# A new order for a hand-scheduled kernel, with 43 DMA transposes instead of 35

## The chip, the core and the metric

The kernel runs on one core of a Trainium2 chip. The core's engines work side by side, each through its own queue in order: TensorE (PE) for matrix products and transposes, VectorE (DVE), ScalarE (ACT) and GpSimd (POOL) for work on elements, and SyncE (SP), which here only issues DMAs. ACT issues DMAs too. An engine that waits for a semaphore holds up all that stands behind it in its queue. The metric is the device time of one execution in microseconds (us). Runs of this kernel lie within about 0.5% of each other.

## What is computed

There are two phases. The first is a recurrent attention with decay; its output, with the heads laid side by side, is the x of the second, a mixing of tokens and channels. Batch 4, 8 heads, 768 positions, head width 64, so x is 4 x 768 x 512.

```python
for t in range(S):
    state = gamma * state + einsum('bhd,bhe->bhde', k[:, :, t], v[:, :, t])
    y[:, :, t] = scale * einsum('bhd,bhde->bhe', q[:, :, t], state)
x = y.transpose(0, 2, 1, 3).reshape(B, S, H * D)
theta = x @ w_theta
zr, zi = x * cos(theta), x * sin(theta)
u = x + einsum('ts,bsd->btd', w_tok_r, zr) + einsum('ts,bsd->btd', w_tok_i, zi)
out = u + maximum(u @ w_ch, 0)
```

The inputs and the output are float32 in HBM; the products are taken in bfloat16.

## The kernel before

The program is a list of short steps, each named by a token in a string, `ORDER` (L23 to L86). The last lines walk through the list and call one function for each token, so the order within each engine's queue is the order of that engine's tokens in the string. Between engines only data and buffers order the work: a token's place among tokens of other engines says nothing of its time. A letter at the end of a token chooses the engine: p for POOL, v for DVE, a for ACT, s for SP's queue.

```python
    for token in ORDER:
        name, *args = token.split(".")
        ops[name](*(int(x) if x.isdigit() else x for x in args))
```

**Attention, 24 units.** A unit n is a batch (n // 6), 256 positions and half of the heads; two units in a row are the two halves of the heads, and three such pairs make a batch. Lk, Lq and Lv (L157) load 256 KB each. ck casts k to bfloat16, cq and cv scale q and v by their decay (L279, L285). k and q must then be transposed, both into the tile kqT: either on PE (Tk and Tq, four transposes each, L293), with E copying the result out of PSUM, or by one DMA of SP, Dk (L309), which reads SBUF and writes SBUF. G.n is PE's main block: the scores of unit n (A, L323), the products of the unit before with its masked scores (Y, L393), and what the unit adds to the state (ST, L351). m.n masks the scores on DVE (L332). SU (L363 to L367) updates the state, SB copies it into bfloat16, and I.n multiplies q with it (L380). XA on ACT (L413) copies a finished part of x, transposed, to SBUF.

**Mixing, 24 tiles C or t of 128 positions** (six of them to a batch). Tx and Ex turn x back by PE and a copy (L427), or Dx does it by DMA (L434). Hh is theta = x @ w_theta (L441), CN its cosine and sine on ACT (L448), z their products with x (L455). Lth and cth bring in w_theta; Lw, cw, Tw and Ew load, cast and transpose the token weights. M.t.s is one part in six of the sum over positions of tile t (L488); it needs z of tile s of the batch. u adds x (L495). Then u is transposed: Tu and Eu by PE and a copy (L500), or Du by DMA (L510). O is u @ w_ch (L515), f adds the rectified product (L521), and SO stores 256 KB (L526). The last tile is cut into halves (Mh, uh, Tuh, Euh, Oh, fh, SOh). warm.n issues n products with zeros while PE has nothing to do.

**Buffers.** kqT has four buffers, uT three, raw loads nine of each kind, and the PSUM banks of most results are single. A transpose by DMA takes a buffer when it is issued, so Du.t waits until the product O that used that buffer is done. The bank of y (M) is single up to t = 17: M.(t+1).0 waits for u.t.

The DMA transposes of the three kinds, which the change touches:

```python
        nc.sync.dma_start_transpose(
            out=kqT.rearrange("p w a j t -> p (w a j) t"),
            in_=st["kqb", n].rearrange("p w d -> p (w d)"))
```

The string ORDER is all that the change edits. The functions that the tokens call are these:

## Time and profile before

| | us |
|---|---|
| median of three runs (169.21 to 170.32) | 170.04 |
| the profiled execution | 170.49 |
| its span, first to last instruction | 168.8 |

| engine | busy in the span, us | share |
|---|---|---|
| PE, matrix products | 156.0 | 92% |
| PE, weight loads | 89.0 | 53% |
| DVE | 123.8 | 73% |
| ACT | 79.2 | 47% |
| POOL | 78.5 | 47% |

The page of the profile has the busy time of each engine, also in 40 slices of the span (4.2 us each), the chain of work that ended last, and groups of like instructions with their mean duration. Queries to the trace give the same for a stretch of time, a line or a tile, a list in order of time, and for DMAs the time from issue to landing. "A <- B" behind an engine's wait names what it waited for. In a group, "128x512 bf16<-128x512 f32" is what is written and read, "x24" the number of instructions. SPq is SP's queue. Matrix products overlap, so a group's mean duration is longer than the distance from one to the next: a product of 128 x 512 has a mean of 379 ns and starts every 0.22 us.

Of the 35 DMA transposes 10 are Dk (units 12, 13, 14, 16, 17, 19 to 23), 11 Dx (tiles 6, 13 to 16, 18 to 23) and 14 Du (tiles 8 to 19, 21, 22). All stand on SP's queue, with the loads and 16 of the 23 whole-tile stores; seven stores are on ACT's.

### The profile page before, as it was taken

The page shows a single profiled execution, that of the slowest core. Times are in us where ns is not written, and L with a number is a line of the kernel's source. Part 1 is how long each engine was busy: PE and PEld are TensorE (multiplying, and loading weights), DVE is VectorE, ACT ScalarE, POOL GpSimd, SP SyncE. Part 2 cuts the span into 40 slices and gives each one's busy share as a digit, 9 for nine tenths or more (in the row PEclk, how much of TensorE's full clock was granted, in tenths as well). Part 3 has the DMA queues.
Part 4 walks back from the last instruction along what each step waited for, and adds up shares of the span by engine and source line. Part 5 has one row for each costly group of instructions (what it writes and reads, how often), then busy time and mean ns, then how long its engine had stood idle before and what let it go on. Part 6 is the DMA issues. An engine that isn't in the chain of part 4 may idle for free.

```text
span 168.8 us, 4924 instructions
## 1 busy us (share of the span) xinstructions
PE 156.0 (92%) x2017; PEld 89.0 (53%) x2044; DVE 123.8 (73%) x200; ACT 79.2 (47%) x159; POOL 78.5 (47%) x99
## 2 busy tenths in 40 slices
PE   7988794989899989999999999999999999999991
...
DMA  4999999999799999999999188899998736335555
GB/s 141 296 290 332 329 322 289 274 319 350 257 283 329 221 232 292 254 207 309 305 244 227 65 188 209 124 276 168 269 230 133 197 62 186 93 93 194 88 188 186
DMA packets 68582, 38.20 MB, mean 226 GB/s; under 512 B 25936, under 2 KB 63056, under 8 KB 68560
## 3 DMA queue, kind: packets, MB, share of 16 engines
...
## 4 chain that ended last, share of the span: by engine, by line
PE 65%; DVE 14%; SPq 11%; DMA 4%; issue 2%; ACT 1%; DVEq 0%; ACTq 0%
PE y_ps L488 31%; PE o_ps L515 11%; PE th_ps L441 9%; SPq L157 9%; DVE z L455 5%; DMA qf<-in_q_dram 4%; DVE at L332 3%; PE at_ps L323 3%; PE r_ps L393 2%; PE r_ps L380 2%; PE y_ps L538 2%; DVE kqb L279 1%; PE kq_ps L293 1%; PE w_ps L472 1%; SPq L185 1%
## 5 line engine op out<-in xcount | busy, mean ns | idle before, releaser
L488 PE MATMUL y_ps<-z,wtr 128*128 128x512 bf16 x135 | 51.2, 379 | 1.0 <-DVE z L455 0.5
L488 PE MATMUL y_ps<-z,wti 128*128 128x512 bf16 x129 | 48.9, 379 | 0.4 <-issue 0.3
L413 ACT CAST xT<-r_ps 128x256 bf16<-128x256 f32 x48 | 16.9, 372 | 30.7 <-PE r_ps L351 19.6
L279 POOL TENSOR_TENSOR kqb<-qf,qsc 128x512 bf16<-128x512 f32 x20 | 23.7, 1189 | 14.1 <-DMA qf<-in_q_dram 13.7
L332 DVE TENSOR_TENSOR at<-at_ps,mask 128x1024 bf16<-128x1024 f32 x24 | 29.1, 1213 | 1.1 <-PE at_ps L323 1.0
L521 DVE SCALAR_TENSOR_TENSOR ot<-o_ps,u 128x512 f32<-128x512 f32 x23 | 15.8, 689 | 14.9 <-PE o_ps L515 14.8
L441 PE MATMUL th_ps<-wth,xT 128*128 128x512 bf16 x89 | 25.0, 395 | 1.4 <-POOL wth L139 1.0
L285 POOL TENSOR_TENSOR vb<-vf,vsc 128x512 bf16<-128x512 f32 x17 | 18.9, 1114 | 10.0 <-DMA vf<-in_v_dram 9.9
L515 PE MATMUL o_ps<-wch,uT 128*128 128x512 bf16 x88 | 23.2, 379 | 0.4 <-DVE wch L139 0.2
L488 PEld LDWEIGHTS <-wti 128*128 128x128 bf16 x138 | 13.5, 98 | 13.4 <-issue 1.1
L448 ACT ACTIVATE cs<-th_ps,halfpi 128x512 bf16<-128x512 f32 x24 | 16.5, 688 | 8.2 <-PE th_ps L441 5.8
L488 PEld LDWEIGHTS <-wtr 128*128 128x128 bf16 x138 | 13.5, 98 | 13.0
L495 DVE TENSOR_TENSOR u<-y_ps,x_sb 128x512 bf16<-128x512 f32 x23 | 15.8, 686 | 5.8 <-PE y_ps L488 5.8
L448 ACT ACTIVATE cs<-th_ps,zerob 128x512 bf16<-128x512 f32 x24 | 16.2, 687 | 5.7 <-PE th_ps L441 5.3
L455 DVE TENSOR_TENSOR z<-cs,x_sb 128x1024 bf16<-128x1024 bf16 x18 | 16.6, 936 | 2.9 <-ACT cs L448 2.7
L455 POOL TENSOR_TENSOR z<-cs,x_sb 128x1024 bf16<-128x1024 bf16 x6 | 12.9, 2153 | 6.6 <-DMA x_sb<-xT 3.9
L139 POOL CAST kqb<-kf 128x512 bf16<-128x512 f32 x16 | 10.6, 666 | 8.3 <-DMA kf<-in_k_dram 6.1
L441 PEld LDWEIGHTS <-xT 128*128 128x128 bf16 x96 | 9.0, 100 | 10.3 <-issue 1.8
L515 PEld LDWEIGHTS <-uT 128*128 128x128 bf16 x92 | 8.7, 98 | 9.5 <-issue 0.3
L137 ACT COPY uT<-u_ps 128x512 bf16<-128x512 bf16 x6 | 3.5, 589 | 21.3 <-PE u_ps L500 21.3
L258 PE MATMUL y_ps<-zero 128*128 128x512 bf16 x36 | 12.0, 447 | 1.4 <-DVE zero L194 1.3
L293 PE MATMUL kq_ps<-ident,kqb 128*128 128x128 bf16 x112 | 9.8, 223 | 2.2 <-DVE kqb L279 2.2
...
## 6 DMA issues: line engine op xcount, KB each, us to landing
...
```

The source lines that it names most:

```text
L157: queues[e].dma_start(out=t.rearrange("p h a d -> p h (a d)"), in_=src[b, h * HU:(h + 1) * HU, i * 2 * P:(i + 1) * 2 * P, :].rearrange("h ...
L279: engines[e].tensor_mul(in_blocks(kqb_of(n)[:, 1]), by_token(raw["qf", n]), _bcast_last(K["qsc"][:, i, :, h * HU:(h + 1) * HU], D))
L285: engines[e].tensor_mul(in_blocks(vb), by_token(raw["vf", n]), _bcast_last(K["vsc"][:, i, :, h * HU:(h + 1) * HU], D))
L332: nc.vector.tensor_mul(at.rearrange("p g j a t -> p (g j) (a t)"), st["at_ps", n].rearrange("p g j a t -> p (g j) (a t)"), _bcast_mid(K["m ...
L413: nc.scalar.copy(st["xT", 2 * i + c][:, 2 * h:2 * h + 2].rearrange("p j (t a) -> p j t a", a=2), st["R", n + 1][:, c, :2 * P].rearrange("p ...
L441: nc.tensor.matmul(th_ps, st["xT", C][:, j, :], K["wth"][:, j, :], start=(j == 0), stop=(j == 3))
L448: nc.scalar.activation(st["cs", C][:, w, :], st["th_ps", C], AF.Sin, bias=K["zerob" if w else "halfpi"], scale=1.0)
L455: engines[e].tensor_mul(st["z", b][:, c], st["cs", C], _bcast_mid(x_of(C), 2))
L488: nc.tensor.matmul(st["y", t], K["wT"][r][:, s0, t0 * P:(t0 + 1) * P], st["z", b][:, s0, r, :], start=(s0 == 0 and r == 0), stop=(s0 == nT ...
L495: nc.vector.tensor_add(st["u", t], st["y", t], st["x", b][:, t0, :])
L515: nc.tensor.matmul(o_ps, st["uT", t][:, j, :], K["wch"][:, j, :], start=(j == 0), stop=(j == nD - 1))
L521: nc.vector.scalar_tensor_tensor(st["ot", t], st["o", t], 0.0, st["u", t], ALU.max, ALU.add)
```

## The change

The order is another one throughout; no function is changed, so the arithmetic is the same. What changes besides the places of the tokens:

| | before | after |
|---|---|---|
| k and q by DMA (Dk) | 12, 13, 14, 16, 17, 19 to 23 | 6, 11 to 15, 17 to 23 |
| x by DMA (Dx) | 6, 13 to 16, 18 to 23 | 11, 12, 14, 16 to 23 |
| u by DMA (Du) | 8 to 19, 21, 22 | 2, 3, 6 to 22 |
| stores SO on SP / ACT | 16 / 7 | 7 / 16 |
| SB on DVE / ACT / POOL | 18 / 23 / 7 | 7 / 25 / 16 |
| ck on DVE / ACT / POOL | 3 / 5 / 16 | 6 / 13 / 5 |
| cv on DVE / POOL | 7 / 17 | 4 / 20 |
| z on DVE / POOL | 18 / 6 | 16 / 8 |
| E on DVE / ACT | 8 / 6 | 6 / 5 |
| Ew on DVE / ACT | 8 / 4 | 6 / 6 |
| products with zeros | 40 | 48 |

The core of the diff, with the stretches that the prediction speaks of:

```diff
...
-const1 const2 const4 const3 const7 warm.8 Lk.0.s Lq.0.s ck.0.p Lv.0.s Lk.1.s const6 Lq.1.s Lv.1.s
-Lk.2.s cv.0.v Lq.2.s ck.1.a cq.0.p Tk.0 warm.4 Tq.0 E.0.v warm.4 G.0 const5 cq.1.v Lv.2.s SU.0
...
-cth.3.a SU.2 cq.4.p cth.2.p SB.2.0.v SB.2.1.v Lk.5.s warm.2 Tk.4 Tq.4 Ex.1.v Lq.5.s Lw.0.0.s
-cth.1.a warm.2 I.2 E.4.v G.3 SU.3 XA.2.1 cth.0.p SB.3.1.a Tx.0 warm.3 Hh.0 SB.3.0.v cv.4.p XA.2.0
-I.3 m.3 cq.5.v CN.0.1 ck.5.p Lv.5.s CN.0.0 cw.0.0.p Ex.0.v Lk.6.s G.4 Tk.5 SU.4 Tq.5 m.4 Lq.6.s
-Lw.1.0.s Hh.1 SB.4.0.a SB.4.1.p E.5.v XA.3.1 Tw.0.0 Lv.6.s cv.5.p Lk.7.s Lq.7.s Ew.0.0.v XA.3.0
-I.4 CN.1.0 Tx.3 ck.6.a G.5 cq.6.v Tq.6 Lv.7.s Lk.8.s CN.1.1 Lq.8.s z.0.p SU.5 SB.5.1.p Tk.6
-cw.1.0.p cv.6.p Lw.0.1.s m.5 Lv.8.s Ex.3.a XA.4.1 Hh.3 XA.4.0 ck.7.p Tx.2 cq.7.p Lk.9.s E.6.v
-Lq.9.s Hh.2 Ex.2.v CN.3.0 ck.8.p SB.5.0.a z.1.v Lw.1.1.s Tw.1.0 Lv.9.s Ew.1.0.v CN.3.1 cq.8.p I.5
-cv.7.p CN.2.0 z.3.v cv.8.p G.6 XA.5.1 Tk.7 XA.5.0 Hh.5 Lk.10.s Tq.7 Tk.8 CN.2.1 m.6 CN.5.1 Lq.10.s
-CN.5.0 SU.6 Hh.4 E.7.v SB.6.1.a Tq.8 SB.6.0.a Tx.4 M.0.0 I.6 cw.0.1.a G.7 z.2.v E.8.v Ex.4.v Tx.5
...
-M.2.1 cq.11.v cq.12.p cv.10.v SU.9 Lv.12.s Lk.13.s Tk.11 XA.8.1 SB.9.1.v M.2.2 Tq.11 cv.12.p M.2.3
-M.2.4 SB.9.0.v ck.13.p Tw.0.3 Dx.6 Lw.0.5.s Lw.1.5.s m.9 M.2.5 Dk.12 E.11.a Tw.1.3 I.9 Lq.13.s
-Lv.13.s cw.0.5.p Ew.0.3.v G.10 Lk.14.s Lq.14.s Ew.1.3.a Tu.0 u.2 SU.10 Eu.0.v M.3.0 M.3.1
-SB.10.0.a Tu.1 cw.0.4.a cw.1.4.v Lv.14.s Lk.15.s Eu.1.v SB.10.1.v M.3.2 XA.9.0 m.10 M.3.3 cch.3.v
-Tx.7 XA.9.1 cq.13.p M.3.4 Ex.7.a M.3.5 Tw.1.4 I.10 Tw.0.4 cch.1.a cch.0.a Dk.13 G.11 Ew.1.4.v
-cch.2.v u.3 Tu.2 O.0 SU.11 Ew.0.4.a ck.14.p Tu.3 cv.14.p XA.10.0 M.4.0 Eu.2.a m.11 M.4.1 f.0
-Eu.3.v z.6.v M.4.2 M.4.3 Lq.15.s SB.11.0.a O.1 M.4.4 cq.14.p XA.10.1 SB.11.1.a M.4.5 Tw.0.5 f.1
...
-Lv.18.s u.5 M.6.0 m.12 M.6.1 CN.10.1 M.6.2 cv.15.p CN.11.1 cq.16.p Ex.10.v I.12 G.13 CN.11.0 M.6.3
-z.10.v Tu.5 XA.12.1 z.11.v Eu.5.a M.6.4 SU.13 M.6.5 SB.13.0.v O.3 u.6 Tu.4 M.7.0 ck.17.p M.7.1
-M.7.2 Dk.16 M.7.3 M.7.4 SB.13.1.a f.3 M.7.5 m.13 Tk.15 Tq.15 XA.12.0 Eu.4.a Lk.19.s E.15.a I.13
-u.7 Lq.19.s G.14 XA.13.0 M.8.0 m.14 SU.14 Lv.19.s XA.13.1 M.8.1 SB.14.0.v M.8.2 SB.14.1.a M.8.3
...
-SO.4.s cv.17.v CN.13.0 z.13.p Eu.6.a I.16 cv.20.p G.17 Dk.19 O.7 SU.17 f.7 Tx.12 SB.17.0.a Tq.18
-Tk.18 Dx.15 M.10.4 XA.16.1 Ex.12.a Lk.21.s O.6 z.12.p XA.16.0 SB.17.1.v ck.20.a M.10.5 cv.19.v f.6
-m.17 SO.5.s u.10 I.17 Hh.15 E.18.a O.8 Du.9 G.18 XA.17.0 f.8 Dx.16 SU.18 ck.21.p Dk.20 Lq.21.s
-M.11.0 m.18 M.11.1 CN.15.1 CN.15.0 cq.21.p M.11.2 Hh.14 Lv.21.s M.11.3 SB.18.0.a XA.17.1 Du.10
-M.11.4 SB.18.1.a Lk.22.s Lq.22.s cq.22.p z.15.v ck.22.p I.18 M.11.5 SO.7.s CN.14.0 G.19 CN.14.1
-Hh.16 u.11 Tx.17 Dk.21 M.12.0 XA.18.0 SU.19 CN.16.0 z.14.v M.12.1 SB.19.0.a Du.11 Hh.17 M.12.2
-M.12.3 Lv.22.s Ex.17.v CN.16.1 XA.18.1 CN.17.0 m.19 SB.19.1.a z.16.v CN.17.1 O.9 I.19 SO.6.s G.20
...
-Du.13 M.20.4 u.22 u.18 M.19.0 O.15 M.17.0 M.19.1 SO.16.a M.17.1 f.15 SO.14.s M.19.2 Du.22 M.19.3
-M.17.2 M.17.3 O.13 f.13 M.17.4 M.17.5 u.17 M.19.4 SO.12.s Du.18 O.18 M.21.0 M.21.1 f.18 M.19.5
-O.22 u.19 Du.17 M.21.2 M.21.3 f.22 SO.15.s M.21.4 Du.19 SO.13.a M.21.5 u.21 Du.21 O.17 M.20.5 f.17
-Mh.0.0 u.20 Mh.0.1 Mh.1.0 Mh.0.2 Mh.0.3 SO.18.a Mh.0.4 Mh.0.5 uh.0 O.19 Tu.20 Mh.1.1 SO.22.s f.19
-Mh.1.2 Eu.20.a Mh.1.3 Mh.1.4 Mh.1.5 uh.1 SO.17.s Tuh.0 O.20 Euh.0 f.20 Tuh.1 O.21 SO.19.s Euh.1
-Oh.0 Oh.1 f.21 SO.20.a SO.21.a fh.0 SOh.0 fh.1 SOh.1
...
+const1 const2 const4 const3 const7 warm.8 const5 Lk.0.s Lq.0.s Lv.0.s Lk.1.s Lq.1.s Lv.1.s cq.1.p
+cq.0.v ck.0.a warm.3 Tq.0 cv.1.p ck.1.a Lk.2.s Lq.2.s Lv.2.s Tk.0 const6 warm.4 Tk.1 E.0.v cv.0.v
+warm.2 G.0 SU.0 SB.0.1.a ck.2.a SB.0.0.a Tq.1 warm.7 I.0 Tk.2 m.0 E.1.v cv.2.v warm.1 G.1 Lk.3.s
+ck.3.a Lq.3.s cq.2.v Lv.3.s SU.1 XA.0.0 SB.1.0.a cq.3.p warm.3 Tq.2 Lk.4.s m.1 Lq.4.s Lv.4.s
+SB.1.1.a Tk.3 cv.3.p E.2.v XA.0.1 warm.5 I.1 cq.4.p ck.4.v Tq.3 Lth.s warm.2 G.2 SU.2 Lk.5.s
+SB.2.1.p m.2 XA.1.0 E.3.a SB.2.0.p Lq.5.s cv.4.p warm.2 Tx.0 Ex.0.a Lv.5.s warm.2 Tk.4 Lk.6.s
...
+SU.3 E.4.v Lv.6.s Lk.7.s XA.2.1 cq.6.p XA.2.0 warm.5 Tq.5 Lq.7.s SB.3.0.a SB.3.1.v m.3 ck.6.v I.3
+ck.5.a G.4 m.4 Lw.0.0.s SU.4 Ex.1.a SB.4.0.v XA.3.0 Hh.1 CN.0.0 ck.7.p CN.0.1 Lw.1.0.s Tk.5 Lv.7.s
+Tx.2 XA.3.1 cq.7.p E.5.v cv.6.p SB.4.1.a I.4 CN.1.0 Dk.6 G.5 CN.1.1 Lk.8.s Lw.0.1.s XA.4.1 z.0.v
+SU.5 Lq.8.s XA.4.0 Ex.2.v SB.5.0.p Lw.1.1.s SB.5.1.a Tx.3 Hh.3 cw.0.0.p CN.3.1 Ex.3.v Tk.7 CN.3.0
+cw.1.0.p Hh.2 m.5 I.5 Tq.7 cv.7.p Lv.8.s Lk.9.s G.6 E.7.a ck.8.a z.1.v SU.6 Tw.0.0 m.6 Lw.0.2.s
+Ew.0.0.v SB.6.0.p Tw.1.0 XA.5.1 Ew.1.0.a Lq.9.s Hh.5 SB.6.1.p z.3.v XA.5.0 Tx.4 CN.2.1 I.6
+cw.0.1.p Ex.4.v CN.2.0 Tx.5 cq.8.p CN.5.0 G.7 CN.5.1 cw.1.1.p Ex.5.v Hh.4 Tk.8 Lv.9.s Tq.8 M.0.0
+Tw.1.1 z.2.v CN.4.1 SU.7 XA.6.1 SB.7.1.p SB.7.0.v cv.8.p CN.4.0 Lk.10.s M.0.1 cw.0.2.p E.8.v
+XA.6.0 m.7 z.4.v M.0.2 cq.9.p M.0.3 I.7 Tw.0.1 Ew.1.1.a G.8 ck.9.a cv.9.p Ew.0.1.v Tw.0.2 M.0.4
+Lq.10.s XA.7.1 Tk.9 Lw.1.2.s z.5.v Lv.10.s SU.8 SB.8.1.v ck.10.p Lw.0.3.s XA.7.0 Tq.9 Ew.0.2.a
+E.9.a Hh.6 Hh.7 M.0.5 m.8 SB.8.0.a CN.7.0 u.0 cw.1.2.v Lk.11.s Lw.1.3.s I.8 CN.7.1 cq.10.p Lch.s
+Lq.11.s Tx.7 G.9 M.1.0 cv.10.v Tx.6 M.1.1 cw.0.3.a Ex.7.v SU.9 M.1.2 SB.9.0.p XA.8.1 Lv.11.s M.1.3
...
+cw.0.4.p Eu.0.a cch.2.v CN.6.1 cch.1.a Tw.1.3 XA.9.0 M.2.0 M.2.1 M.2.2 M.2.3 Lk.13.s Ew.1.3.v
+Tw.0.3 cq.12.p ck.11.a SU.10 Ew.0.3.a SB.10.1.a m.10 M.2.4 M.2.5 Tu.1 Dk.11 u.2 XA.9.1 O.0 Tx.8
+Eu.1.a M.3.0 Lq.13.s M.3.1 z.6.v Ex.8.a M.3.2 Tx.9 Lv.13.s SB.10.0.a ck.12.v f.0 Tw.0.4 z.7.v
+cw.1.4.a Lw.0.5.s Lw.1.5.s Ex.9.v Ew.0.4.v cv.12.p Lk.14.s M.3.3 M.3.4 M.3.5 cq.13.p I.10 ck.13.a
+O.1 G.11 Dk.12 Tw.1.4 f.1 Hh.9 u.3 XA.10.0 SU.11 cv.13.p Ew.1.4.a cw.0.5.v cw.1.5.p SB.11.0.v
+XA.10.1 CN.9.0 CN.9.1 m.11 Hh.8 M.4.0 Tw.0.5 M.4.1 Lq.14.s ck.14.a M.4.2 Ew.0.5.v Du.2 SB.11.1.p
+Tw.1.5 I.11 CN.8.1 CN.8.0 M.4.3 Dk.13 Lv.14.s G.12 XA.11.1 M.4.4 Ew.1.5.a m.12 SU.12 M.4.5 cq.14.v
+u.4 z.9.p SB.12.1.p SB.12.0.a Lk.15.s Hh.11 cv.14.p XA.11.0 O.2 Tx.10 I.12 G.13 M.5.0 Lq.15.s
+Dk.14 M.5.1 M.5.2 Dx.11 XA.12.0 m.13 CN.11.1 SU.13 M.5.3 z.8.p CN.11.0 SB.13.1.a f.2 M.5.4 Du.3
+M.5.5 SB.13.0.a u.5 XA.12.1 Lv.15.s Hh.10 CN.10.1 I.13 G.14 Ex.10.v cq.15.p ck.15.v CN.10.0 M.6.0
...
+Dk.15 O.3 cq.16.p Tu.4 M.7.0 cv.15.p M.7.1 SB.14.0.a Lk.17.s M.7.2 SB.14.1.a Lq.17.s m.14 f.3
+M.7.3 Eu.5.a Lv.17.s Lk.18.s Lq.18.s SO.0.a Tk.16 Eu.4.v cv.16.p XA.13.0 I.14 Lv.18.s SO.1.s G.15
+M.7.4 M.7.5 Lk.19.s O.4 Tq.16 XA.14.1 SU.15 Tx.13 u.7 SB.15.1.a M.8.0 cv.17.p m.15 f.4 cq.17.v
+M.8.1 E.16.a XA.14.0 SB.15.0.a M.8.2 M.8.3 M.8.4 Lq.19.s ck.17.p I.15 G.16 SU.16 O.5 SO.2.s M.8.5
+f.5 Hh.13 u.8 Dk.17 XA.15.1 Hh.12 Ex.13.v m.16 SB.16.1.p M.9.0 cq.18.p Tx.15 SO.4.a SB.16.0.p
+M.9.1 XA.15.0 M.9.2 CN.13.0 Du.7 M.9.3 CN.12.0 Du.6 cq.19.p I.16 CN.12.1 ck.19.v G.17 M.9.4 SO.3.a
+Dx.12 M.9.5 CN.13.1 u.9 ck.18.p Hh.15 SU.17 O.7 cv.18.p Du.8 M.10.0 M.10.1 Dk.18 f.7 SB.17.1.a
+M.10.2 Ex.15.v z.12.p O.6 Lv.19.s SB.17.0.a XA.16.0 M.10.3 XA.16.1 Lk.20.s m.17 f.6 I.17 Lq.20.s
+G.18 z.13.p SU.18 Lv.20.s XA.17.1 O.8 M.10.4 f.8 Dk.19 Dx.14 CN.15.0 ck.20.a Dx.17 XA.17.0 m.18
+SB.18.0.a CN.15.1 cv.19.p M.10.5 Hh.17 SB.18.1.v Hh.14 cq.20.p I.18 u.10 G.19 z.15.p CN.14.0
+M.11.0 CN.14.1 SU.19 m.19 Lk.21.s Dk.20 SB.19.1.a M.11.1 M.11.2 Dx.16 M.11.3 XA.18.0 SB.19.0.a
+Lq.21.s Lv.21.s cv.20.p ck.21.p Du.9 z.14.v M.11.4 M.11.5 Du.10 XA.18.1 u.11 CN.17.1 Lk.22.s I.19
+Hh.16 cq.21.p SO.5.a G.20 M.12.0 CN.16.0 XA.19.1 CN.16.1 M.12.1 Hh.19 m.20 z.16.v M.12.2 Dk.21
...
+u.14 I.21 M.16.0 m.21 f.11 M.16.1 M.16.2 ck.23.a M.16.3 Lv.23.s cv.22.p cq.23.p Dx.18 M.16.4 Dx.19
+M.16.5 Dk.23 Hh.18 u.16 G.22 SU.22 cv.23.v CN.18.0 M.15.0 SB.22.1.p CN.18.1 Du.12 XA.21.1
+SB.22.0.v m.22 M.15.1 z.19.p M.15.2 Du.16 Hh.21 SO.9.a SO.8.s XA.21.0 I.22 Hh.20 G.23 CN.20.0 m.23
+CN.20.1 Dx.20 M.15.3 SU.23 z.18.p SO.11.s M.15.4 Dx.21 XA.22.0 M.15.5 SO.10.a O.16 XA.22.1 M.20.0
+u.15 f.16 SB.23.1.a Du.14 SB.23.0.p M.13.0 M.13.1 O.12 f.12 I.23 CN.21.0 M.13.2 CN.21.1 G.24
+z.20.v XA.23.0 M.13.3 XA.23.1 z.21.v M.13.4 M.20.1 Dx.23 M.20.2 M.22.0 Hh.22 M.22.1 M.13.5 Hh.23
...
+M.19.0 M.19.1 O.15 M.19.2 M.17.0 f.15 M.17.1 M.19.3 Du.18 M.17.2 M.17.3 O.13 f.13 M.19.4 SO.15.a
+Du.22 M.17.4 M.17.5 SO.14.a O.18 M.19.5 u.17 f.18 u.19 Du.17 M.20.5 M.21.0 SO.13.a O.22 M.21.1
+f.22 SO.18.a M.21.2 SO.22.a Du.19 M.21.3 O.17 M.21.4 u.20 M.21.5 f.17 Du.20 O.19 u.21 Mh.0.0 f.19
+Mh.1.0 Mh.1.1 Mh.0.1 Du.21 Mh.1.2 Mh.1.3 Mh.1.4 Mh.1.5 uh.1 Mh.0.2 Mh.0.3 Mh.0.4 Mh.0.5 Tuh.1 uh.0
+O.20 SO.19.a Euh.1 Tuh.0 SO.17.a O.21 Euh.0 f.20 SO.20.a f.21 Oh.0 Oh.1 fh.0 fh.1 SO.21.a SOh.1
+SOh.0
 """.split()
```

## The prediction

> **What bounds the kernel now.** I read the page's slices first, to find where TensorE (PE) is the limit, then a table by stage, then PE's waits, then the costs of the operations that are exchanged, and last SyncE's queue where it runs late.
>
> ```profile
> PE 156.0 (92%) x2017; PEld 89.0 (53%) x2044; DVE 123.8 (73%) x200; ACT 79.2 (47%) x159; POOL 78.5 (47%) x99
> PE   7988794989899989999999999999999999999991
> DMA  4999999999799999999999188899998736335555
> ```
>
> ```profile
> 0.00:40.00 40.00, 33.18 (x559) 20.09 (x568) 30.77 (x53) 23.09 (x45) 29.09 (x52) 0.96 1.04 293
> 40.00:100.00 60.00, 58.39 (x847) 35.34 (x856) 52.49 (x83) 34.20 (x69) 31.20 (x34) 1.00 1.08 248
> 100.00:130.00 30.00, 29.63 (x419) 15.83 (x422) 23.53 (x38) 14.25 (x32) 12.36 (x13) 1.00 1.02 202
> 130.00:169.00 39.00, 34.84 (x212) 17.70 (x200) 17.03 (x28) 7.69 (x15) 5.88 (x3) 1.00 0.51 142
> ```
>
> The columns of the table are the stretch, then PE, weight loads, VectorE (DVE), ScalarE (ACT), GpSimd (POOL), clock, DMA share, GB/s. From 40 us on, PE is busy 122.9 of 129 us, and some 4 of the other 6 are the tail after its last matmul. So it sets the end: what PE is spared there is gained, and every new PE wait is lost. Up to 40 us the loads set the pace (293 GB/s, DMA share over 1), and PE's busy time holds 12.0 us of warm-up (the group at L258).
>
> ```profile
> PE kq_ps L293 <- DVE kqb L279: 2.2, 1, 2.2
> ...
> PE th_ps L441 <- POOL wth L139: 1.0, 1, 1.0
> ```
>
> Those are two of PE's longest waits (total, times, longest), both in the first 30 us; the waits after 40 us come to 1.4 us in all.
>
> ```profile
> 47.13 0.22 PE kq_ps L293 x4
> ...
> 96.25 0.22 PE u_ps L500 x4
> ```
>
> ```profile
> L309 SPq DMA_TRANSPOSE kqT<-kqb x10: 1232/1414/4040, 58.2 to 123.6; - x10
> ...
> DMA to landing us min/median/max: 4.3/4.7/6.6
> ```
>
> The first two lines, from the chain that ended last, give the price of a group of four transposes on a busy PE: 0.22 us. The others give its replacement: 1.2 to 4.0 us (median 1.4) of SyncE's queue, and 4.3 to 6.6 us until the data lie there. For x (L434) and u (L510) the same view shows 1.2 us, and 2.4/3.4/6.3 and 2.4/3.3/5.4 to landing.
>
> ```profile
> 104.73 1.19 SPq L434 DMA_TRANSPOSE x_sb<-xT  x1
> 106.01 1.26 SPq L309 DMA_TRANSPOSE kqT<-kqb  x1
> 107.32 1.22 SPq L157 DMA_DIRECT2D qf<-in_q_dram  x1
> ...
> 112.37 1.39 SPq L309 DMA_TRANSPOSE kqT<-kqb  x1
> ```
>
> ```profile
> 111.30 1.04 POOL L279 TENSOR_TENSOR kqb<-qf,qsc 128x512 bf16<-128x512 f32 x1 [5.53 <-DMA qf<-in_q_dram]
> ```
>
> Here SyncE runs late: POOL waits 5.53 us for a load that stood behind two transposes, and the next transpose (Dk.21) waits for POOL. Dk.21 landed 5.7 us after its issue, at 118.0, and PE began the unit's scores at 119.53: it did not wait, but the margin was 1.5 us.
>
> **The Trainium skill.** "Perfetto Trace Analysis", section "Per-instruction lifecycle", says that a DMA instruction's window leaves out the data movement: the trace agrees, 1.4 us beside 4.7. "DMA: Bandwidth & Descriptors", section "Issuing engines are not separate DMA queues", says that issuing from another engine saves the sequencer's time alone: so the stores moved to ACT relieve SyncE and not the DMA engines; no run here shows that yet. "TensorE: Matmul & The Clock Gate", section "Part 4: PE-mode transpose", has about 275 ns for one transpose in a kernel; the trace's records are 223 ns, but four take 0.22 us together, and that measurement decides. "SBUF — State Buffer", section "SBUF: two separate sides", says that a DVE operation with two SBUF inputs and a GpSimd one exclude each other for a whole instruction. The trace agrees: cq.6 on DVE ran 26.32 to 28.74, 2.42 us against 0.69 for an undisturbed one, and ended 0.57 us after a POOL product (26.05 to 28.17).
>
> **The change, step by step.** All against the profiled execution's 170.49 us (span 168.8, 1.7 around it), which is 0.45 above the median of 170.04.
>
> 1. *Transposes off PE.* k/q: units 6, 11, 15, 18 go to DMA, 16 comes back: 3 pairs of four. u: 2, 3, 6, 7, 20. x: 6, 13, 15 come to PE, 11, 12, 17 leave: zero. So 6 + 5 = 11 groups of 0.22 us: **-2.4 us**. Their evictions go too (DVE 0.42 and 0.68, ACT 0.59 and 1.0), which with SB moved mainly to POOL (DVE's SB 18 to 7) relieves DVE by some 9 us of 124; DVE ended no PE wait after 40 us beyond about 1 us, so at nothing (cover: PE's own queue of work).
>
> 2. *The front.* Lw.0.0 and Lw.1.0 now stand behind Lq.7, so Lq.6 has 0.39 MB less ahead: at 293 GB/s 1.3 us earlier, landing at 25.0 instead of 26.3. cq.6 moves to POOL (1.04 to 1.2): done near 26.2, and the 2.2 us wait goes. What is late next is Dk.6: its issue waits for cq.6, and behind it on SyncE are Lk.8 and all later loads. In the loading stage a load lands 6 us after issue, so I take 6.4 (bounds 4.3 and 8): 32.7. Scores of unit 6 (G.6) began at 33.5 before, so 0.7 earlier. Behind it the order now has two weight transposes, I.6, Tx.5 and G.7 before M.0.0: 4.8 us of PE work plus about 1 us in which Tx.4 and Hh.4 wait for ACT (XA.5.0, CN.2): M.0.0 near 38.7 against 37.9, with 0.7 us more work done (I.6 0.12, G.7 0.79, Tx.5 0.22, less Tk.6 and Tq.6 0.44). Hh.6, Hh.7 and Tw.0.2 come forward to fill the wait for z.5 (Hh 0.86 each, Tw 0.34): M.0 ends near 45.8 against 43.9 with 1.6 us more done. **+0.3 us** (-1 to +1.5: later loads stand 1.7 us or more further back, Tq.8 and Tq.9 queue on them). Hh.0's wait for theta weights moves with Lth, one load later (0.9 us), under eight more warm-ups; in the same bounds.
>
> 3. *SyncE.* Added: 3 x 1.4 + 5 x 1.2 = 10.2 us; nine stores leave, 9 x 0.5 = 4.5 us. ACT takes them at 0.35 each, 3 us, at 47% busy: nothing. Most of the addition lies between 60 and 100 us, where SyncE waits for producers anyway.
>
> 4. *New PE waits.* The order brings units 11 to 18 forward: between G.12 and G.14 stand 8.1 us of PE work instead of 15.6, between M.5.5 and G.15 7.9 instead of 15.6 (sums: M 0.43, Hh and O 0.86, G 0.8, I and four transposes 0.22). Held against the chain that must pass meanwhile, with 0.1 us per hand-over, an estimate:
>  - G.14: scores 0.35, m.12 1.21, SU 0.57, cq.14 on DVE 1.15, Dk.14 4.7, hand-overs 0.4 = 8.4 against 8.1: 0.3 late.
>  - G.15: u.5 0.69, Ex.10 0.41, ck.15 0.70, Dk.15 4.7, hand-overs 0.4 = 6.9 against 7.9: late only above 5.7; 0.2.
>  - G.21: the chain shown above, but between the release by XA.17 and Lq.21 stand also Dx.17 (1.19) and Lk.21 (0.58): 1.8 longer, while G.18 to G.21 is 16.2 us of PE work against 16.0. The margin of 1.5 becomes -0.1; with the spread 0.6.
>  - G.20, G.22, G.23: margins near 1 us or below: 0.1, 0.2, 0.3.
>  - M.20.0: z.19 and z.18 now run one after the other on POOL (2.15 each) behind SB.22.1: 6.3 against 7.0 of PE work: 0.1.
>  - O.21 in the tail: Du.21 reuses the buffer that O.19 frees, then 2.4 to 3.8 us; O.21 is due 3.7 us after O.19: 0.1.
>  Sum **+1.9 us**, taking the median landing. With 4.3 everywhere about 0.5; with 5.7 to 6.6 about 5, since a wait early gives margin later. Below nothing is excluded: a transpose that is in time gains nothing more.
>
> Sum: -2.4 + 0.3 + 1.9 = -0.2, so 170.3 for this execution and **169.8 us** on the scale of the runs.
>
> **Rivals.**
> *The transposes land in time.* For it: 14 DMA transposes of u and 10 of k/q were all in time before, and SyncE has 4.5 us of stores fewer. Then -2.4 + 0 + 0.2: 167.8 us. Against: up to 100 us the margins of k/q were then 4 to 8 us, and are about 1 us now.
> *The transposes land late (slower).* One mechanism: a kqT block that lands after PE has reached its scores holds the whole in-order PE queue. The longest landings (6.6, one issue of 4.0 us) were found where loads and stores were in flight; now 43 transposes share that stretch. With five of the seven places late by 0.9 us and the loads behind Dk.6 costing 0.8: -2.4 + 0.8 + 4.5 = +2.9, so 172.9 us. It decides once new waits and the front together exceed 4.1 us (2.4 and 1% of 170). Against: stalls add margin behind them.
>
> **How the numbers follow.** 1% (1.7 us) is about what a measurement of this kernel can tell from no change. Forecast, within 1%: 0.40. In time, faster: 0.24. Late, slower: 0.36. The range reaches from the fast rival's 167.8 to the slow one's 172.9, a little over the latter for the bound of the landings: 167.6 to 173.4. Within the forecast's own case it is 168.4 to 171.4.
>
> **What would show it.** PE's kq_ps groups at 88 instead of 112, u_ps at 16 instead of 36, SyncE transposes 13, 11 and 19. PE's wait for DVE kqb L279 gone; new PE waits at L323 or L380 on kqT<-kqb (DMA), near 33, 74, 81 and 115 to 127 us: none means the fast rival, over 4 us the slow one. POOL still waits for qf and vf after 100 us. Step 2 is wrong if M.0 ends before 44.5 or after 47.5; step 1 if the busy sum of transposes falls by other than 44 instructions. The forecast fails if DMA landings change (median beyond 4.3 to 5.7), or if a wait appears on an engine that I costed at nothing: DVE, POOL or the stores on ACT.

## Result and the profile after

The changed kernel takes **175.49 us** (median of 4 runs, 175.27 to 176.2) beside 170.18 us (169.21 to 171.73) for the kernel before on the same chip: a ratio of 1.031 (95% interval 1.0227 to 1.0394). It is slower by 5.3 us, above the range of the prediction. The profiled execution took 175.62 us, with a span of 173.6 us, 4.8 more than before. The ratios leave out executions more than 1.5% above the fastest of their kernel and the medians do not, so the two can differ by a per cent: what is concluded below rests on the ratios, and a cost in us is the ratio less one, times the time of before on the same chip.

The page of the kernel after, busy times and slices (a slice is 4.3 us):

```profile
PE 156.8 (90%) x2008; PEld 85.4 (49%) x2008; DVE 109.4 (63%) x185; ACT 81.9 (47%) x164; POOL 79.8 (46%) x101
PE   7799795799999999999999997769998999999991
DMA  4999999999999999969999989999999946164545
```

The table by stage, columns as before:

```profile
0.00:40.00 40.00, 32.79 (x564) 18.92 (x564) 27.32 (x50) 24.16 (x48) 23.04 (x47) 1.00 1.06 268
40.00:100.00 60.00, 58.90 (x833) 33.94 (x832) 43.37 (x77) 36.64 (x73) 33.51 (x36) 1.00 1.11 266
100.00:130.00 30.00, 25.72 (x352) 13.07 (x351) 17.23 (x28) 12.46 (x27) 15.83 (x14) 1.00 1.03 215
130.00:173.60 43.60, 39.41 (x264) 19.48 (x262) 21.48 (x32) 8.68 (x18) 7.43 (x5) 0.98 0.60 149
```

The new hole lies between 100 and 130 us: TensorE is idle 4.3 us there, against 0.4 before. The DMA share of that stretch is as before (1.03 and 1.02), and up to 40 us data come at 268 GB/s instead of 293. PE's waits (total, times, longest) name what was late:

```profile
PE at_ps L323 <- DMA kqT<-kqb: 4.1, 4, 1.2
...
PE o_ps L515 <- DMA uT<-u: 1.8, 1, 1.8
...
PE r_ps L380 <- ACT sbd L137: 1.6, 1, 1.6
```

The wait for DVE's kqb is gone; kqT from DMA has taken its place at 34.0, 107.2, 112.8 and 133.7 us, uT from DMA at 117.6, and at 28.8 us I.4 waits for the copy SB.4.1, which the change moves from GpSimd to ACT. Two lines of POOL's waits for q, first before, then after, show that its supply of loads worsened too; the load of q of unit 20 landed at 94.5 us before and at 105.4 after:

```profile
POOL kqb L279 <- DMA qf<-in_q_dram: 13.7, 7, 5.5
```

```profile
POOL kqb L279 <- DMA qf<-in_q_dram: 27.2, 12, 5.1
```

SyncE's queue in the kernel after (start, time to issue, instruction) shows what stood ahead of them:

```profile
101.79 2.54 SPq L309 DMA_TRANSPOSE kqT<-kqb  x1
104.43 2.53 SPq L434 DMA_TRANSPOSE x_sb<-xT  x2
107.02 0.57 SPq L157 DMA_DIRECT2D kf<-in_k_dram  x1
107.76 2.88 SPq L309 DMA_TRANSPOSE kqT<-kqb  x1
110.73 1.22 SPq L434 DMA_TRANSPOSE x_sb<-xT  x1
112.00 0.57 SPq L157 DMA_DIRECT2D qf<-in_q_dram  x1
112.63 0.50 SPq L157 DMA_DIRECT2D vf<-in_v_dram  x1
113.23 2.75 SPq L510 DMA_TRANSPOSE uT<-u  x2
```

From 89.2 to 138.8 us SyncE issues without a break (before, from 95.8 to 122.5). Dk.19 has its block at 94.9 and is issued at 101.8, u of tile 9 is ready at 97.8 and issued at 113.2, and Lq.21 stands behind three transposes. Once issued, the transposes landed about as fast as before (in the median 5.0 us for k and q against 4.7, and 3.5 for u against 3.3), so it is the issue that came late. The view of L309 in the kernel after:

```profile
L309 SPq DMA_TRANSPOSE kqT<-kqb x13: 1232/1515/3068, 26.1 to 129.1; - x13
...
DMA to landing us min/median/max: 3.6/5.0/7.9
```

ACT was held up as well. The store of tile 5, whose data were ready at 92.2 us, stands in ACT's order at 112.81 us, 0.02 us after kqT of unit 20 landed, and the trace names that landing as what ended ACT's wait of 2.88 us:

```profile
112.81 0.34 ACTq L526 DMA_DIRECT2D out_dram<-ot  x1
113.25 0.69 ACT L448 ACTIVATE cs<-th_ps,halfpi 128x512 bf16<-128x512 f32 x1 [2.88 <-DMA kqT<-kqb]
```

Here TensorE waited for the same kqT. In each of the twelve profiles with the middle of the new order a store held ACT for 1.9 to 3.7 us, always one of the tiles 0, 3, 4 and 5, whose stores the change moves from SyncE to ACT; in the order of before only that of tile 9 does so, for 1.4 to 2.0 us.

**A measure for the runs below.** "Lost" is the time of a point less the TensorE work done by then, which is the number of each operation times its distance to the next one when nothing waits (M 0.43, Hh and O 0.86, G 0.70, Tw 0.34, I 0.22 or 0.12, a group of four transposes 0.22, the warm-ups none). All values are us, from one profiled execution each:

| kernel | work | lost by 50 | 50 to 100 | 100 to end |
|---|---|---|---|---|
| before | 140.9 | 21.7 | 1.7 | 0.5 |
| after | 138.5 | 23.0 | 2.2 | 5.9 |
| before, seven transposes added | 138.7 | 19.8 | 6.3 | 2.4 |
| before, four added, Du.6 early | 139.6 | 21.5 | 1.7 | 2.8 |
| before, front filled | 140.9 | 20.2 | 1.5 | 2.0 |
| after, loads on ACT | 138.5 | 22.3 | 1.8 | 5.2 |
| after, all loads early | 138.5 | 23.4 | 6.3 | 1.6 |
| after, late SyncE order | 138.5 | 22.5 | 3.9 | 5.1 |
| after, late loads early | 138.5 | 23.5 | 4.4 | 4.1 |
| order alone | 140.7 | 22.2 | 2.8 | 4.4 |
| order alone, Dx.17 later | 140.7 | 23.9 | 2.8 | 2.4 |
| order alone, loads early | 140.7 | 23.8 | 3.9 | 2.0 |
| front of before, rest of after | 138.9 | 22.3 | 2.5 | 2.4 |
| front of after, rest of before | 140.5 | 23.9 | 1.8 | 0.8 |

Work and loss make the last product's end; some 4 us of tail follow. Eight kernels that are alike up to 50 us have lost 22.2 to 23.9 by then, so differences under 1.5 us between two traces tell nothing here. Their mean is 23.1, that of the three with the front of before (the first, third and fourth lines) 21.0: the front costs some 2 us. The whole of it is: 2.4 us of work saved, as predicted, and 7.2 us more lost, in this pair of traces 1.3 in the front and 5.9 after it.

### The profile page after: what moved, and what is told of

Same layout as the page of the kernel before. It is cut to its first block, busy times and chain, and to the rows that moved or that the text cites. A ratio compares the mean times of both kernels' runs of the same rounds, so it can differ in the third digit from the quotient of the medians.

```text
span 173.6 us, 4907 instructions
## 1 busy us (share of the span) xinstructions
PE 156.8 (90%) x2008; PEld 85.4 (49%) x2008; DVE 109.4 (63%) x185; ACT 81.9 (47%) x164; POOL 79.8 (46%) x101
## 4 chain that ended last, share of the span: by engine, by line
PE 33%; DMA 30%; SPq 22%; DVE 6%; POOL 3%; issue 2%; ACT 2%; DVEq 0%; POOLq 0%; ACTq 0%
PE y_ps L488 16%; SPq L157 16%; DMA kqT<-kqb 10%; PE o_ps L515 8%; DMA vf<-in_v_dram 5%; DMA out_dram<-ot 4%; SPq L309 4%; DMA wtok<-in_moe_w_tok_r_dram 3%; DMA qf<-in_q_dram 3%; DMA kf<-in_k_dram 3%; PE th_ps L441 3%; DMA uT<-u 2%; DVE z L455 2%; SPq L510 2%; PE y_ps L538 2%
## 5 line engine op out<-in xcount | busy, mean ns | idle before, releaser
L488 PE MATMUL y_ps<-z,wtr 128*128 128x512 bf16 x138 | 52.4, 380 | 0.0
L488 PE MATMUL y_ps<-z,wti 128*128 128x512 bf16 x138 | 52.3, 379 | 0.0
L279 POOL TENSOR_TENSOR kqb<-qf,qsc 128x512 bf16<-128x512 f32 x20 | 21.3, 1064 | 27.7 <-DMA qf<-in_q_dram 27.2
L285 POOL TENSOR_TENSOR vb<-vf,vsc 128x512 bf16<-128x512 f32 x20 | 22.4, 1122 | 10.3 <-DMA vf<-in_v_dram 10.1
L455 POOL TENSOR_TENSOR z<-cs,x_sb 128x1024 bf16<-128x1024 bf16 x8 | 16.9, 2122 | 13.4 <-DMA x_sb<-xT 13.2
L455 DVE TENSOR_TENSOR z<-cs,x_sb 128x1024 bf16<-128x1024 bf16 x16 | 14.7, 930 | 3.5 <-ACT cs L448 3.5
L258 PE MATMUL y_ps<-zero 128*128 128x512 bf16 x48 | 14.4, 422 | 1.3 <-DVE zero L194 1.3
L323 PE MATMUL at_ps<-kqT 64*64 64x128 bf16 x384 | 10.0, 222 | 4.2 <-DMA kqT<-kqb 4.1
L137 ACT CAST kqb<-kf 128x512 bf16<-128x512 f32 x13 | 8.1, 621 | 9.0 <-DMA kf<-in_k_dram 8.8
L137 ACT CAST sbd<-s 64x256 bf16<-64x256 f32 (+1 forms) x25 | 9.0, 360 | 6.1 <-DVE s L363 2.9
```

The costliest lines, as they stand in the source:

```text
L137: nc.scalar.copy(dst, src)
L279: engines[e].tensor_mul(in_blocks(kqb_of(n)[:, 1]), by_token(raw["qf", n]), _bcast_last(K["qsc"][:, i, :, h * HU:(h + 1) * HU], D))
L285: engines[e].tensor_mul(in_blocks(vb), by_token(raw["vf", n]), _bcast_last(K["vsc"][:, i, :, h * HU:(h + 1) * HU], D))
L455: engines[e].tensor_mul(st["z", b][:, c], st["cs", C], _bcast_mid(x_of(C), 2))
L488: nc.tensor.matmul(st["y", t], K["wT"][r][:, s0, t0 * P:(t0 + 1) * P], st["z", b][:, s0, r, :], start=(s0 == 0 and r == 0), stop=(s0 == nT ...
```

## Experiments

Theories: **1** SyncE's in-order queue is too full; **2** the 16 DMA engines are; **3** the front (Dk.6); **4** the new order itself; later **5**, the place of single instructions on SyncE's queue.

### The changed kernel with one suspect relieved

```diff
-... Lv.19.s Lk.20.s Lq.20.s Lv.20.s ... Lv.23.s
+... Lv.19.a Lk.20.a Lq.20.a Lv.20.a ... Lv.23.a
```

> The kernel after, with 13 loads of units 19 to 23 (Lv.19 to Lv.23, in use from about 99 to 126 us) issued from ScalarE's queue instead of SyncE's, at the same places of the order. The DMA engines carry the same bytes; SyncE is spared 13 x 0.55 = 7 us of issuing in the stretch from 89 to 139 us, which it issues through without a break. Theory 1 (SyncE's in-order queue is too full there, so kqT and uT come late): PE's waits after 100 us fall from some 7 us to below 3, and the time from 175.5 to 170.5 to 172.5 us. Theory 2 (the DMA engines themselves are too full; 43 transposes take longer to land whoever issues): no more than 1 us is gained, 174.5 to 176. Theory 3 (the loss is in the first 50 us, behind Dk.6): no change, 175 to 176.

174.78 us (173.56 to 181.74), ratio 1.0288 (1.0071 to 1.0505), an interval too wide to tell a gain. PE's waits for kqT fell from 4.1 to 1.3 us and those for uT vanished, but TensorE stood 3.9 us between 100 and 120 us, hardly less than in the changed kernel (4.2): now for xT from ACT (1.3 us at Hh.19, behind a store that held ACT for 3.7 us), z from DVE and others. SyncE's queue held up those blocks; with it relieved, other waits took their place.

```diff
-CN.1.0 Dk.6 G.5 ... SB.5.1.a Tx.3 Hh.3
+CN.1.0 G.5 ... SB.5.1.a Tq.6 Tk.6 Tx.3 E.6.v Hh.3
```

> The kernel after, with unit 6 transposed by PE again (Tq.6, Tk.6, eviction on VectorE) in place of Dk.6. PE has 0.44 us more work. Theory 3: the kernel after is behind because Dk.6 lands at 34.0, 7.9 us after its issue, and because the loads queue behind it; then scores of unit 6 come 2 us or more earlier, M.0 ends 1.5 to 2.5 us earlier, and if nothing downstream takes it back the time is 173 to 174. Theory 1: SyncE's queue from 89 us on does not depend on PE's first 50 us alone, so part of the gain is lost again in longer waits there: 174 to 175.5.

175.7 us (174.34 to 178.39), ratio 1.0318 (1.0173 to 1.0462): no gain that can be told, and none of the four executions reached theory 3's 173 to 174 us, though the interval includes them. Dk.6 does cost the loads something: from 26 to 36 us ten profiles with it moved 223 to 294 GB/s (mean 261), this one 343. TensorE did not get further for it in this trace, but that is of the slowest execution (178.39 us), with a low clock behind the wait at I.4 (1.7 us lost). So what Dk.6 costs stays open.

### The transposes alone, in the order of before

```diff
-... Tk.11 Tq.11 E.11.a ... Tk.15 Tq.15 E.15.a ... Tk.18 Tq.18 E.18.a
-... Tu.2 Eu.2.a ... Tu.3 Eu.3.v ... Tu.6 Eu.6.a ... Tu.7 Eu.7.a
+... Dk.11 ... Dk.15 ... Dk.18 ... Du.2 ... Du.3 ... Du.6 ... Du.7
```

> The kernel before, with its own order and engines, in which only seven more blocks are transposed by DMA: k/q of units 11, 15 and 18, u of tiles 2, 3, 6 and 7, put on SyncE's queue where their data are ready and 4 us or more ahead of their use. PE is spared 10 groups of four transposes, 10 x 0.22 = 2.2 us. If moving transposes to DMA is sound in itself and the new order's thin margins are the fault: 168 to 169 us. Theory 1: three of the seven (Dk.18, Du.6, Du.7, some 5 us of issuing) fall into the stretch where SyncE runs late already, all later loads and transposes move back by up to 5 us against margins of 1 to 2.5 us, and PE waits 1 to 4 us: 169.5 to 172. Theory 2: similar to theory 1, but with landings of transposes and loads longer than before by 0.5 us or more in the median.

173.32 us (171.8 to 176.19), ratio 1.0174 (1.0039 to 1.031). In the trace one wait did most of it: 2.83 us for unit 11, whose transpose took 4.25 us to issue among loads. Behind it the granted clock fell. Theory 2's sign is missing: the transposes landed 4.3 us (k and q) and 3.1 us (u) after their issue in the median, before 4.7 and 3.3. With the loads of units 20 to 23 on ACT's queue as well:

```diff
-... Lv.20.s ... Lk.21.s ... Lv.23.s
+... Lv.20.a ... Lk.21.a ... Lv.23.a
```

> The kernel of e5_dma_alone with 10 loads (Lv.20 to Lv.23) issued from ScalarE's queue. SyncE is spared 10 x 0.55 = 5.5 us between 97 and 121 us, about what the three transposes added. Theory 1: PE's waits after 100 us vanish, and the 2.2 us of PE work that is saved comes through: 167.5 to 169. Theory 2: same as e5_dma_alone within 0.7 us.

180.77 us (179.81 to 181.11), ratio 1.0634 (1.0541 to 1.0727), far from theory 1's forecast, but for another reason: TensorE waited 3.6 us for uT and 3.77 for ACT, which stood 4.93 us in front of a load that the trace has waiting for a store. Theory 1 is not tested by it. Two runs with four of the transposes, the second with Du.6 issued when its data were there:

```diff
-... Tk.15 Tq.15 E.15.a ... Tk.18 Tq.18 E.18.a ... Tu.6 Eu.6.a ... Tu.7 Eu.7.a
+... Dk.15 ... Dk.16 Du.6 ... Du.7 ... Dx.14 Dk.18
```

> The kernel before with four of the seven transposes given to DMA (k/q of 15 and 18, u of 6 and 7) and nothing else changed: 6 groups of 0.22 us leave TensorE, 1.3 us; 5.2 us come to SyncE's queue between 75 and 98 us. If in the run with all seven the loss came from the one wait for unit 11's block at 57 to 60 us and the lower clock after it, this gives 168.9 to 169.5 (faster than before). If it came from the amount of transposes on SyncE or on the DMA engines, it gives 170.5 to 172.

> The kernel before with k/q of 15 and 18 and u of 6 and 7 by DMA, as in the run with these four, only u of tile 6 is given to SyncE right behind Dk.16, some 83 us, and no longer behind Du.8 and a store at 95.6 us (its data were there at 78 us). If the loss of that run was this one wait (2.9 us, and 1.7 us by the lower clock behind it), this gives 168.5 to 169.5, faster than before by the 1.3 us of the six groups. If the amount of transposes is the cause, 170.5 to 172.

172.09 us (ratio 1.0125, 1.0064 to 1.0186), where Du.6 stood behind Du.8 and a store, and 172.7 us (1.0194, 1.0128 to 1.026) with it early. In the first TensorE waited 2.91 us for Du.6. In the second that wait is gone and no PE wait over 2.2 us is left, but 2.3 us more than before are lost after 100 us, in waits of 0.3 to 0.6. The forecast of 168.5 to 169.5 failed: removing the wait moved the loss. Both times are near the 170.5 to 172 us that were expected if the amount of transposes is the cause. No set of added transposes paid in the order of before: +3.0, +2.1 and +3.3 us by the ratios.

### The place of instructions on SyncE's queue

Same instructions, another order on SyncE's queue. First 18 loads earlier, of which those ahead of Dk.15 matter below; then, from 88 us on, loads earlier and the transposes in the order of their use; then only the loads from 88 us on, with Dx.17 later. The stretch of each:

```diff
-SO.2.s Dk.17 Du.7 Du.6 Dx.12 Du.8 Dk.18 Lv.19.s Lk.20.s Lq.20.s Lv.20.s Dk.19 Dx.14 Dx.17 Lk.21.s
+SO.2.s Lv.19.s Lk.20.s Lq.20.s Dk.17 Du.7 Du.6 Dx.12 Du.8 Lv.20.s Lk.21.s Dk.18 Lq.21.s Lv.21.s Dk.19
```

(the third), and of the first two

```diff
-Dk.14 Dx.11 Du.3 Lv.15.s Lk.16.s Lq.16.s Lv.16.s Dk.15 Lk.17.s Lq.17.s Lv.17.s
+Lv.15.s Lk.16.s Dk.14 Dx.11 Du.3 Lq.16.s Lv.16.s Lk.17.s Lq.17.s Lv.17.s Dk.15
...
-SO.2.s Dk.17 Du.7 Du.6 Dx.12 Du.8 Dk.18 Lv.19.s Lk.20.s Lq.20.s Lv.20.s Dk.19 Dx.14 Dx.17 Lk.21.s
+SO.2.s Lv.19.s Lk.20.s Dk.17 Du.7 Dx.12 Lq.20.s Du.6 Dk.18 Lk.21.s Du.8 Dk.19 Lq.21.s Lv.20.s Dx.14
```

> The changed kernel with the same instructions; only on SyncE's queue 18 loads (of units 14 to 22) stand earlier, ahead of the transpose of k and q that they stood behind (so that a transpose that waits for its block doesn't hold them up). The DMA engines move the same bytes. Theory 1 (SyncE's queue, its waits among them) expects most of the late 5.4 us back: 171 to 172.5, and POOL's wait for loads at L279 down from 27.2 us to under 12. Theory 2 (the DMA engines are full) expects 174.5 to 176: what is loaded earlier is transposed later. Theory 4 (order of TensorE's work) expects 175.

> The changed kernel with the same instructions; only on SyncE's queue, from the store of tile 2 to the load of v of unit 23, the order is another: the loads of units 19 to 23 two to six places earlier, and the transposes in the order of their use (Dk.19, Dk.20 and Du.9 earlier, Dx.14, Dx.16, Dx.17 and Du.10 later). Unlike the run with all loads moved, nothing changes before 88 us. Theory 1 (what is late is late since it stands in the wrong place of a full queue of SyncE's) expects the waits at G.19, G.20 and O.9 (5 us) to go and 171 to 172.5. Theory 2 (the DMA engines or SyncE's whole amount of work are the limit, whatever the order) expects other waits in their place and 174.5 to 176.

> The changed kernel with the same instructions; on SyncE's queue only the loads of units 19 to 22 from 88 us on stand earlier (as in the run with all loads moved, but none of those that had delayed the transpose of unit 15), and Dx.17, which waits for its blocks, stands behind Du.10 and no longer ahead of Lk.21. Theory 5 (what is late after 100 us is what stands behind a transpose that waits or takes long on SyncE's in-order queue, loads above all, so the place decides and not the amount) expects the idle time of TensorE from 100 to 140 us to fall from 4.8 to under 1.5 us and 171.5 to 173. Theories 1 and 2 (the amount of transposes for SyncE or the DMA engines) expect it elsewhere again and 174.5 to 176.

175.57 us (ratio 1.0319, 1.0257 to 1.0381), 174.87 us (1.0347, 1.0269 to 1.0426) and 175.07 us (1.029, 1.0227 to 1.0353). With all loads early, the loss after 100 us falls from 5.9 to 1.6, and 4.1 us appear before 100, above all at G.15, whose transpose now stands behind five loads. In the second the waits at G.19, G.20 and O.9 are gone; others of 0.4 to 1.4 us stand at G.17, O.6, M.12.5, O.10 and O.16. In the third it is the block of unit 17 that TensorE waits for (2.3 us), as its waits show (L322 there is L323 in the kernel after):

```profile
PE at_ps L322 <- DMA kqT<-kqb: 5.0, 4, 2.3
```

Every repair made something else late, and the total stayed at 175 us: theories 1 and 5, which expected 171 to 173, failed. Theory 2 names such a sum that doesn't move, but the times to landing above and the next runs speak against it.

### The order alone

The seven transposes go back to TensorE, some 2 us ahead of their use:

```diff
-Dk.11 ... Du.2 ... Du.3 ... Dk.15 ... Du.7 ... Du.6 ... Dk.18
+Tk.11 Tq.11 E.11.a ... Tu.2 Eu.2.a ... Tu.3 Eu.3.a ... Tk.15 Tq.15 E.15.a ... Tu.7 Eu.7.a ... Tu.6 Eu.6.a ... Tk.18 Tq.18 E.18.a
```

> The changed order with the seven transposes that it adds in the middle (k/q of units 11, 15, 18; u of tiles 2, 3, 6, 7) back on TensorE, some 2 us ahead of their use: 3 x 2 + 4 = 10 groups of 0.22 us, so 2.2 us more TensorE work than the changed kernel, and 9 us less on SyncE. Theory 1 (SyncE's in-order queue is too full between 89 and 139 us) and theory 2 (the 16 DMA engines are too full) both expect about 170.5: the 5.4 us of late waits go, 2.2 us of work and the 1.8 us of the front stay. Theory 4 (the new order itself leaves too little work between a block's making and its use, whoever transposes the other blocks) expects 174 to 176, with waits of 3 us or more for kqT from DMA left between 100 and 136 us.

179.57 us (176.48 to 181.74). Its median tells little, since a cast on DVE took 7.28 us in its trace and TensorE waited 2.96 us for what stood behind it; the fastest execution is as long as those of the mended kernel:

```diff
-ck.19.v ... M.3.4 Tk.11 Tq.11 M.3.5 E.11.a
+ck.19.a ... M.3.1 Tk.11 Tq.11 ... Ex.8.a E.11.a
```

> The changed order with the seven transposes of k/q 11, 15, 18 and u 2, 3, 6, 7 back on TensorE, as in the first run of this kind, without its two accidents: the cast of k of unit 19 goes to ACT (on DVE it took 7.28 us beside GpSimd's products, and TensorE waited 2.96 us for what stood behind it), and unit 11 is transposed before a tile of x whose buffer it waited for. TensorE has 2.2 us more than in the changed kernel. Theories 1 and 2 (transposes by DMA are too many for SyncE or for the DMA engines): 170.5 to 171.5. Theory 4 (the order alone): 173.5 to 175.

**176.36 us** (175.88 to 177.86), ratio 1.0467 (1.0404 to 1.053): the order alone, with its choice of engines, is at least as slow as the whole change, with one DMA transpose more than before (36; it keeps Dk.6 and the changed set of x). So the added transposes are not what the change loses by. But theory 4's sign, late kqT, is missing too: the waits at G.19, G.20 and G.23 went with the seven transposes, as theory 1 has it, and in their place stand I.14 (0.95 us, behind the store of tile 0, which held ACT for 2.2) and I.22 (1.4 us, up to the end of SB.22.0, which took DVE 2.2 us beside a product z on GpSimd). O.9 (1.8) stayed. Its SyncE queue, columns as above:

```profile
97.09 3.01 SPq L309 DMA_TRANSPOSE kqT<-kqb  x1
100.14 7.08 SPq L434 DMA_TRANSPOSE x_sb<-xT  x2
107.27 0.58 SPq L157 DMA_DIRECT2D kf<-in_k_dram  x1
...
111.84 1.27 SPq L510 DMA_TRANSPOSE uT<-u  x1
```

Of the 7.08 us SyncE stood 4.4 at Dx.17, waiting for a block that is used at 117 us, and u of tile 9, ready at 99.1 and due at 115.8, came behind it. So these four went ahead of Dx.17 and Dk.20:

```diff
-Dk.19 Dx.14 Dx.17 Lk.21.s Dk.20 Dx.16 Lq.21.s Lv.21.s Du.9 Du.10
+Dk.19 Dx.14 Du.9 Lk.21.s Lq.21.s Lv.21.s Dk.20 Dx.16 Du.10 Dx.17
```

> The kernel with the order alone (seven transposes on TensorE), with one change on SyncE's queue: Du.9, Lk.21, Lq.21 and Lv.21 stand ahead of Dx.17 and Dk.20, which wait there for their blocks (SyncE stood from 101.7 to 106.0 us at Dx.17, with these four ready behind it). Theory 5 expects the wait of 1.8 us at O.9 to go, and with the loads 5 us earlier those at G.20 to G.23 too: 172.5 to 174 instead of 176.4. If the cost of the order lies elsewhere (too little work between the steps of a unit), 175.5 to 177.

174.95 us (173.88 to 176.47), ratio 1.027 (1.0193 to 1.0346): the wait at O.9 is gone and the loss after 100 us is down from 4.4 to 2.4, yet of 7.9 us over before (on another chip) 4.6 remain. It is between the two forecasts: the place on the queue was part of the cost and not the most of it.

The order alone with the loads placed as in the third order above:

```diff
-SO.2.s Dk.17 Dx.12 Du.8 Lv.19.s Lk.20.s Lq.20.s Lv.20.s Dk.19 Dx.14 Dx.17 Lk.21.s
+SO.2.s Lv.19.s Lk.20.s Lq.20.s Dk.17 Dx.12 Du.8 Lv.20.s Lk.21.s Lq.21.s Lv.21.s Dk.19
```

> The kernel with the order alone, with the loads of units 19 to 22 earlier and Dx.17 later, as in the changed kernel with late loads moved. Against that one it has 2.2 us more on TensorE and seven transposes fewer on SyncE. Theory 5 expects 172.5 to 173.5, within 1 us of that one (the transposes cost in waits about what they spare). If the amount of transposes counts for more than their 2.2 us, this is faster than that one by 2 us or more.

176.16 us (174.62 to 178.69), ratio 1.0312 (1.0244 to 1.0381). The forecast of 172.5 to 173.5 failed; that it would lie within 1 us of the kernel with late loads early held, which had 1.029 on the same chip. So in the new order the seven transposes are worth 0.4 us here, of the 2.2 us that they take off TensorE (2.6 by the ratios of the whole change and of the order alone, from two chips). I.14 waits 1.8 us, behind the store of tile 0 on ACT (3.0).

And the changed kernel with that order of loads and two steps of the front undone:

```diff
-SB.4.0.v ... SB.4.1.a I.4 CN.1.0 Dk.6 G.5 ... Tx.3 Hh.3
+SB.4.0.v SB.4.1.v ... I.4 CN.1.0 G.5 ... Tq.6 Tk.6 Tx.3 E.6.v Hh.3
```

> The changed kernel with late loads moved and Dx.17 later, and the front undone in two places: k and q of unit 6 are transposed on TensorE again, and the copy SB.4.1 that the inter-chunk product I.4 waits for goes from ACT to DVE. If the front costs the changed kernel the 1 to 2 us that its trace shows by 40 us, this is 1 to 2 us faster than the run without the undoing: 170 to 171.5. If the loads set the pace there whatever is done, the same time.

176.61 us (173.7 to 177.94), ratio 1.0215 (1.0129 to 1.0301). By the ratios it is 1.3 us faster than the kernel with late loads early on the same chip (1.029), as expected if these two steps are what the front costs. But the ratio rests on two executions of five, the intervals overlap, and the profile is of one of the other three. So the cost of Dk.6 and of the copy on ACT is not shown either way.

### The two halves of the order

Both orders were cut at M.0.0 (38 us) and joined crosswise: every token not yet used follows in the other order.

```diff
-order = before
+order = before[:M.0.0] + [t for t in after if t not in it]
...
-order = before
+order = after[:M.0.0] + [t for t in before if t not in it]
```

> The kernel before up to its first product of z with the token weights (M.0.0, 38 us), then all that is left in the order of the changed kernel: its front undone, with 42 of the 43 transposes by DMA. If the time that TensorE had lost by 50 us (23.0 us in the changed kernel, 20.2 and 21.7 in two profiles of the order before) is paid at the end, this is some 2 us faster than the changed kernel: 172.5 to 173.8. If the late waits take up whatever the front gives, since they hang on the loads and not on TensorE, 174.5 to 176.

> The other half: the changed kernel up to M.0.0, then all that is left in the order of the kernel before, with its transposes by DMA and unit 6: 36. If the front's loss is paid at the end, 172.5 to 173.8, and the two halves together come to the 5 us of the whole. If only the rest of the order costs, the time of before within 0.7 us.

**173.43 us** (171.76 to 174.72), ratio 1.0232 (1.0167 to 1.0296), and **172.52 us** (171.03 to 174.74), ratio 1.0156 (1.0087 to 1.0225). The rest costs 3.9 us (2.8 to 5.0) with its transposes and the front 2.6 (1.5 to 3.8), together 6.5; the whole costs 5.3 (3.9 to 6.7), so within the noise the halves add up to it. With the front of after the loads land later, and PE waits where the order before had no such wait, for q of unit 9:

```profile
PE kq_ps L293 <- POOL kqb L279: 2.3, 2, 2.1
```

The late waits seem to hang on the front: the same rest loses 2.4 us after 100 us behind the front of before, and 5.9 behind its own, in one trace of each (the former of the fastest of its executions).

### The clock behind a wait, and more DMA work

```diff
-I.4 CN.1.0 Tx.3 ck.6.a G.5 cq.6.v Tq.6
+I.4 CN.1.0 Tx.3 ck.6.a G.5 warm.9 cq.6.v Tq.6
```

> The kernel before with nine products of zeros (0.22 us each) ahead of the transposes of q of unit 6, where TensorE stands for 2.2 us until 28.8 us; no other change. If waits of 2 us and more set the granted clock to 0.5 for some 3.3 us (as at 29.7 to 33.1 us in the profile of before, 1.7 us lost), the clock stays at 1.0 there and this gives 168.3 to 169.3. If the lower clock in that place costs nothing (since the loads set the pace up to 40 us), the time of before within 0.5 us.

169.72 us (median of 22, 168.23 to 171.66) beside 170.83 (of 28, 167.87 to 173.39); ratio 1.0021 (0.9983 to 1.0058): no difference that can be told. The 28 runs spread by 3%, not by the 0.5% of the first three. The row from 30 to 35 us, before and then with the wait filled (clock third from the end):

```profile
30.00:35.00 5.00, 4.95 (x74) 3.21 (x74) 3.60 (x6) 2.92 (x7) 5.00 (x7) 0.68 1.01 287
```

```profile
30.00:35.00 5.00, 4.67 (x82) 2.85 (x82) 4.96 (x9) 4.25 (x10) 4.96 (x6) 1.00 1.05 299
```

The clock stays up and 1.5 us less are lost by 50 us, but 1.5 us more are lost after 100, 1.1 of them in a wait at G.23. No version beat the kernel before.

For theory 2 the kernel before got loads that nobody reads:

```diff
+def LX(n):
+    t = io.tile([P, HU, 2, D], FT, name="xf", bufs=2)
+    nc.scalar.dma_start(out=t.rearrange("p h a d -> p h (a d)"),
+        in_=k[0, 0:HU, 0:2 * P, :].rearrange("h (p a) d -> p h (a d)", a=2))
...
+... ck.13.p LX.1 ... Eu.1.v LX.0 ... M.4.3 LX.2 ... ck.15.p LX.3 ... Dk.17 LX.4 ... Dx.14 LX.5
```

> The kernel before with six further loads of 0.25 MB into a tile that nobody reads, on ACT's queue (0.35 us each there), where the change adds its transposes between 56 and 98 us; SyncE's queue is as before. Theory 2 (the DMA engines' time) expects landings 0.5 us or more longer and 172.5 to 174; theory 1 and theory 4 expect the time of before, within 0.7 us.

175.99 us (175.96 to 176.57), ratio 1.0371 (1.032 to 1.0422), and it doesn't tell what it was made for: 5 of the 6.3 us come from one place, where ACT stood 4.8 us at the issue of such a load until 62.1 us, PE waited 3.3 us for it and then ran at half clock. So theory 2 is not tested by itself.

## Why the prediction was wrong

**Step 1 held.** Work fell by 2.4 us, and the products into kq_ps and u_ps are 88 and 16.

**Step 2 failed in size.** It put the front at +0.3 with bounds of -1 to +1.5; in times the front alone is +2.6. Dk.6 landed 7.9 us after its issue (6.4 taken, 8 the bound), and M.0's last step began at 46.8 us, inside the bounds named, though the wait at Tq.6 and the 1.7 us of lower clock behind it had gone. That later loads stand back by 1.7 us or more was named and left inside the bounds: k of unit 8 landed at 34.9 us instead of 31.6, q of unit 9 at 42.8 instead of 35.8, k of unit 10 at 44.6 instead of 38.5. With unit 6 back on TensorE they landed at 31.3, 37.9 and 39.6. The step had no term for the 1.6 us that I.4 waits for SB.4.1 on ACT. What each of these makes of the 2.6 us is not shown.

**Step 3 failed: it put SyncE's added work and the stores on ACT at nothing.** It counted issue times and took 60 to 100 us as the stretch that matters. A transpose of k and q took 1.5 us in the median and up to 3.1, and whatever stands behind one that waits or takes long is late with it: loads, then POOL's products, then the next Dk. Loads made POOL wait 27.2 us for q instead of 13.7. A store's issue itself took ACT 0.34 us as counted, but a store that waited for a DMA of SyncE's queue to land held ACT for up to 3.7 us.

**Step 4 was right in kind and too small.** +1.9 was forecast, and 5.9 us more were lost after 50 us. Of the eight places that it priced, G.20 was late by 1.2 us (0.1 forecast), G.23 by 0.5 and G.22 by 0.1; G.14, G.15, G.21, M.20.0 and O.21 were in time. That these come to 1.8 us is luck. G.19 (1.2) and O.9 (1.8) were not foreseen. The chains were priced one by one from their own steps, with loads taken as there and SyncE as free to issue.

**The rivals.** The slow one named the sign (kqT late, over 4 us of such waits: 4.1), at 172.9. Its cause, longer landings with more transposes in flight, is not the main one: they landed in 5.0 us, and the order without seven of them is as slow. The fast one fell in the order of before too, where three sets of transposes cost 2.1 to 3.3 us each.

**Left open:** which moves of the new order, or of its choice of engines, make the 4 to 5 us that stay when single waits on SyncE's queue are mended, and which steps of the front make its 2.6 us. No run puts the stores of tiles 0, 3, 4 and 5 back on SyncE's queue.
